# Second-stage matrix in four pieces, loads in shorter runs, and all projection tiles ahead of the last transform

## The chip, the cores and the metric

The kernel runs on one core of one Trainium2 chip. The metric is the device time of one execution, in microseconds. Names used below: TensorE (PE, matmul), VectorE (DVE), ScalarE (ACT), GpSimd (POOL) and SyncE (SP, which only issues transfers here).

## What is computed

The reference mixes two branches for a sequence of S = 2048 rows and D = 640 channels, with a gate for each row:

```python
x = A_q
g = sigmoid((x * gate_w).sum(-1, keepdims=True))
a = q * (causal_fft_conv(k_shift * v, ssm_k) + (k_shift * v) * ssm_D)     # FFT length 2*S
b = attention(x @ wqkv) @ wo          # 32 heads of 20, 8 keys at a distance of 2
return g * a + (1 - g) * b
```

k_shift is a four-tap convolution of k along the sequence. The long convolution is done with transforms written as matmuls: a first stage (F1b), a second stage (G), the product of the transformed filter h and the transformed data kv, then a first inverse stage (M) and a second inverse stage (T). The second branch is local attention with its output projection by wo.

## The kernel before

One program holds all parts, and a small list scheduler written into the kernel decides the order of instructions: each part is a generator that asks for an engine with an estimated cost and with events to wait for. The order is fixed when the program is built; each engine then works through its own stream in order. PSUM is divided into four slots; a part takes one or two of them and gives them back when the copy out of PSUM is done.

The loads, all issued by SyncE in this order (the part from the stores of kv on):

```python
yield from store_kv(3)
yield from store_kv(2)
yield from load_h(0)                     # first half of the filter, runs of 128 bytes
yield from store_kv(1)
yield from store_kv(0)
yield from load_h(1)                     # second half, 8 transfers
yield from load("G", G, cf["G"]..., 2097152, 16384, [ev("stg21"), ev("stg30"), ev("stg31")])
for c in range(2):
    yield from load(f"kv{c}", kvs[:, 5120 * c:5120 * (c + 1)], ..., 1310720, 10240, stored)
yield from load("wo", ...)
```

G lies in the tile Gs, which earlier holds staging for the q and k projections; GpSimd copies that staging by DMA into the head-wise tiles qb and kb ("fragger"). `stg21`, `stg30` and `stg31` are the events that the last of those copies are done.

A second-stage unit of the transform (there are 4 for each of 5 groups, for the filter "h" and for the data "u"):

```python
def s2_unit(dst, jb, Am, deps, free):
    r = yield Req("P", 680.0, deps + [ev("G")], take=1)
    ps = psum(r, "s2")
    for jj in range(8):
        j = 8 * jb + jj
        for rr in range(2):
            for c in range(2):
                ...
                nc.tensor.matmul(o, lhsT=G[rows, j, rr, :], rhs=Am[rows, 2 * j + rr, :, :], ...)
    e = yield Req("AD", n=1024, deps=[r.done, free], give=r.banks)     # copy out, ScalarE or VectorE
```

The load of q (for the product with the gate) and its scaling, the second inverse stage, and the output projection:

```python
def load_q():
    yield Req("G", 1.0, [ev("us1")])              # after the last reader of kv, whose place qg takes
    for g in range(4):
        r = yield Req("G", 700.0, move=us(655360, 20480))
        nc.gpsimd.dma_start(st["qg"][32 * g:32 * g + 32], raw(x2, 16 * g * D, [[64 * D, 32], [1, 16 * D]]))
    mark("qg", r)

def qscale():                                     # 16 tiles, VectorE: q times the gate
    for t in range(16):
        r = yield Req("D", 230.0, [ev("qg"), ev("gate")])
        ...

def inverse2():                                   # groups of 3 tiles: 96 matmuls, then two copies and two products
    for t0 in range(0, 16, 3):
        g = yield Req("P", m * 32 * 16.0, [ev("Cm"), ev("T"), ev("qg"), ev("gate")], take=2)
        ...

def outproj():                                    # 16 tiles of 40 matmuls
    for t in range(16):
        late = [ev(f"pr{t}")] if t >= EARLY else []        # EARLY = 12
        g = yield Req("P", 1510.0, late, take=1, pri=None if t < EARLY else 0)
        ...                                       # copy out times (1 - gate) into bl
        # t < 12: added two tiles at a time by early_adds; t >= 12: added one by one, then stored
```

So the last four projection tiles stand behind the second inverse stage; `pr{t}` is the event that tile t has its product with q.

Of the kernel before, what the change touches and what calls it, by code (L numbers as in the profile page):

```python
# [12 lines left out]
ACT = mybir.ActivationFunctionType  # L13
ALU = mybir.AluOpType
# [3 lines left out]
S = 2048  # L18
D = 640
# [16 lines left out]
GROUPS = [[0, 1, 2, 3], [4, 5, 6, 7], [8, 9, 10], [11, 12, 13], [14, 15, 16]]  # L36
PARTS = [((0, 1), [(0, 8)]), ((2, 3, 4), [(8, 5), (13, 4)])]

EARLY = 12
AHEAD = 2  # L40

NG = 5
# [179 lines left out]
def kernel(  # L222
# [105 lines left out]
    def loads():  # L328
# [45 lines left out]
        yield from load("G", G, cf["G"].ap().rearrange("p (a r b) -> p a r b", a=32, r=2), 2097152, 16384,  # L374
                        [ev("stg21"), ev("stg30"), ev("stg31")])
        stored = [ev(f"st{a}{c}") for a in range(4) for c in range(2)]
        for c in range(2):
            yield from load(f"kv{c}", kvs[:, 5120 * c:5120 * (c + 1)], raw(kv_scr[:], c * 4 * S * 80, [[5120, 128], [1, 5120]]), 1310720, 10240, stored)
# [291 lines left out]
        return e.done  # L670

    def s2_unit(dst, jb, Am, deps, free):
        r = yield Req("P", 680.0, deps + [ev("G")], take=1)
        ps = psum(r, "s2")
        for jj in range(8):
            j = 8 * jb + jj
            for rr in range(2):
                for c in range(2):
                    rows = slice(64 * c, 64 * c + 64)
                    o = ps[:, c, :].rearrange("p (q j l) -> p q j l", q=4, j=8)[:, :, jj, :]  # L680
                    nc.tensor.matmul(o, lhsT=G[rows, j, rr, :], rhs=Am[rows, 2 * j + rr, :, :],  # L681
                                     start=(rr == 0), stop=(rr == 1), tile_position=(64 * c, 0), skip_group_check=True)
# [222 lines left out]
    def outproj():  # L905
        yield Req("G", 1.0, [ev("oT"), ev("wo"), ev("gate")])
        oT, wo, bl = st["oT"], st["wo"], st["bl"]
        for t in range(16):
            late = [ev(f"pr{t}")] if t >= EARLY else []
            g = yield Req("P", 1510.0, late, take=1, pri=None if t < EARLY else 0)  # L910
            op = psum(g, "op", (128, 1024))
            for ft in range(NDT):
                a = oT[:, ft, 0:1]
                for n0, n1 in ((0, 512), (512, 640)):
                    for gg in range(4):
                        nc.tensor.matmul(op[32 * gg:32 * gg + 32, n0:n1],  # L916
                                         lhsT=raw(a, HS * (t % 2) + t // 2 + 8 * gg, [a.ap[0], [32, 32]]), rhs=wo[:, ft, n0:n1],
                                         start=(ft == 0), stop=(ft == NDT - 1), tile_position=(0, 32 * gg), skip_group_check=True)
            r = yield Req("AD", dict(A=725.0, D=880.0), [g.done] + late, give=g.banks)
            if t >= EARLY and r.eng == "D":  # L920
                qg = st["qg"]
                nc.vector.scalar_tensor_tensor(qg[:, t, :], op[:, 0:D], omg[:, t:t + 1], qg[:, t, :], op0=ALU.mult, op1=ALU.add)
            else:
                if r.eng == "A":
                    nc.scalar.activation(bl[:, t, :], op[:, 0:D], ACT.Copy, scale=omg[:, t:t + 1])  # L925
                else:
                    nc.vector.tensor_scalar(bl[:, t, :], op[:, 0:D], omg[:, t:t + 1], None, ALU.mult)
                if t >= EARLY:
                    qg = st["qg"]
                    yield Req("D", 410.0, [r.done])  # L930
                    nc.vector.tensor_tensor(qg[:, t, :], qg[:, t, :], bl[:, t, :], ALU.add)
            mark(f"bl{t}", r)
            if t >= EARLY and t % 2 == 1:
                store(t)
# [38 lines left out]
    plan.add(load_t(), 0)  # L973
    plan.add(load_q(), 1)
    plan.add(qscale(), 4)
    plan.add(early_adds(), 2)
    plan.add(inverse2(), 0)
    plan.run()

# [29 lines left out]
```

## Time and profile before

The time before is 275.25 us, the median of 3 runs (273.52 to 278.2). The profiled execution has a span of 273.6 us.

| stretch of the span, us | TensorE busy | VectorE | ScalarE | granted clock | DMA share |
|---|---|---|---|---|---|
| 84 to 104 | 18.91 of 20.00 | 10.69 | 18.69 | 1.00 | 0.67 |
| 104 to 114.6 | 8.26 of 10.60 | 7.90 | 10.11 | 0.71 | 0.97 |
| 114.6 to 122.7 | 0.08 of 8.10 | 0.62 | 1.58 | 0.50 | 0.99 |
| 122.7 to 147 | 22.04 of 24.30 | 16.91 | 19.64 | 0.50 | 0.24 |
| 147 to 160 | 9.03 of 13.00 | 8.58 | 9.46 | 0.76 | 0.99 |
| 212 to 226 | 10.97 of 14.00 | 7.75 | 9.35 | 0.95 | 0.60 |
| 226 to 240 | 12.22 of 14.00 | 10.65 | 9.39 | 0.93 | 0.30 |
| 240 to 252 | 6.11 of 12.00 | 7.50 | 7.50 | 0.71 | 0.28 |
| 252 to 262 | 8.62 of 10.00 | 5.44 | 5.04 | 0.67 | 0.61 |

The table is made from the busy time of each engine in stretches of the span. The granted clock is the share of full speed at which TensorE was let run. The DMA share is how busy the 16 transfer engines were. Transfers that matter here, from issue to landing: G 14.0 us (2048 KB), kv 17.5 us (median of two, 1280 KB each), q 11.1 us (median of four, 640 KB each), the filter 4.1 us (median of sixteen, 160 KB each).

How to read the profile's lines: a timeline row gives the start, the duration, the engine, the line of the program, the operation, what it writes and reads (out<-in), its shape and how many instructions are merged; in square brackets stands the idle time of the engine ahead of it and what ended that ("<-issue" where nothing that the profile shows was waited for). The chain of work that ended last is followed back from the last instruction.

### The profile page before, as it was taken

To read this page: it belongs to the slowest core of one execution; us is meant where nothing else is said; L and a number is where in the kernel's file an instruction comes from. 1 tells how busy PE (TensorE), PEld (TensorE's weight loads), DVE (VectorE), ACT (ScalarE), POOL (GpSimd) and SP (SyncE) were. 2 spreads that over 40 slices of the span, in tenths; PEclk is the share of its full clock that TensorE was granted. 3 is DMA by queue.
4 is the path that set the end of the run, shared out by engine and by line. 5 is a ranking of instruction groups with operands and counts; after the bars stand their busy time and mean duration, and the time that the engine had idled before them with its cause. 6 is when DMAs were issued, how large, how long until landed. Compare 5 with 4: busy or idle time off the path is not lost.

```text
span 273.6 us, 10626 instructions
## 1 busy us (share of the span) xinstructions
PE 219.5 (80%) x4825; PEld 164.2 (60%) x4825; DVE 178.0 (65%) x224; ACT 180.3 (66%) x219; POOL 59.5 (22%) x123
## 2 busy tenths in 40 slices
PE   1899999999999998508989496979999959845920
PEld 1675665555656666407869395868787848833510
DVE  0289189999998546606678566867749558747520
ACT  1155567887887999907888642867979755666420
POOL 7701534760702374200000000000000200012420
PEclk9999999999999999555555959999999998995595
DMA  6999899868930698997004966510400196005640
GB/s 202 300 376 415 279 224 74 203 176 158 211 84 14 185 158 148 272 333 298 7 2 98 230 145 151 128 32 5 156 6 2 41 206 143 2 18 127 145 110 0
DMA packets 40525, 40.11 MB, mean 147 GB/s; under 512 B 26544, under 2 KB 35888, under 8 KB 39200
## 3 DMA queue, kind: packets, MB, share of 16 engines
q1 hardware_dynamic: 36208, 29.41, 40.8%
q0 software_dynamic: 4272, 10.02, 16.0%
q8 instruction: 38, 0.62, 1.0%
q14 instruction: 7, 0.06, 0.1%
HBM read 23.50 MB, written 5.25 MB: 105 GB/s over the span
## 4 chain that ended last, share of the span: by engine, by line
PE 58%; issue 11%; DVE 11%; DMA 8%; ACT 7%; POOL 1%; POOLq 0%; SPq 0%; DVEq 0%; ACTq 0%
PE pj L530 12%; PE psv L478 8%; PE op L916 8%; PE i L808 7%; PE s L681 7%; DMA Gs<-cf_G 5%; DVE Am L251 4%; PE s L663 4%; ACT ET L604 3%; PE O L630 3%; PE sc L596 3%; PE tr L831 2%; PE trx L460 2%; DVE X L794 2%; DVE Hs L791 2%
## 5 line engine op out<-in xcount | busy, mean ns | idle before, releaser
L604 ACT ACTIVATE ET<-sc 128x726 bf16<-128x726 f32 (+1 forms) x80 | 64.3, 865 | 10.9 <-PE sc L596 10.6
L530 PE MATMUL pj<-xT,Wqk 128*128 128x363 bf16 (+3 forms) x250 | 48.2, 343 | 0.6 <-DVE oS L644 0.6
L681 PE MATMUL s<-Am,Gs 64*128 64x64 bf16 x1280 | 31.3, 205 | 19.6 <-issue 10.8
L681 PEld LDWEIGHTS <-Gs 64*128 64x128 bf16 x1280 | 27.4, 105 | 24.5 <-issue 14.8
L251 DVE CAST Am<-s 128x1024 bf16<-128x1024 f32 x27 | 32.4, 1222 | 13.0 <-PE s L663 12.9
L530 PEld LDWEIGHTS <-Wqk 128*128 128x128 bf16 x250 | 23.0, 97 | 19.0 <-DVE oS L644 0.8
L916 PE MATMUL op<-wo,Hb 128*32 128x512 bf16 (+1 forms) x640 | 27.4, 323 | 2.2 <-issue 1.5
L478 PE MATMUL psv<-Wv,xT 128*128 128x320 bf16 x170 | 26.7, 309 | 1.6 <-DVE xT L251 1.0
L249 ACT CAST X<-i 128x1024 bf16<-128x1024 f32 x20 | 20.2, 1012 | 9.3 <-PE i L808 9.3
L846 POOL DMA_DIRECT2D qg<-in_A_q_dram x4 | 2.0, 509 | 101.8 <-PE s L681 101.8
L916 PEld LDWEIGHTS <-Hb 128*32 128x32 bf16 x640 | 17.8, 139 | 9.1 <-issue 4.5
L808 PE MATMUL i<-M,X 128*128 128x128 bf16 x160 | 22.1, 233 | 0.4 <-DVE X L794 0.4
L478 PEld LDWEIGHTS <-xT 128*128 128x128 bf16 x170 | 16.4, 100 | 8.7 <-issue 1.7
L808 PEld LDWEIGHTS <-X 128*128 128x128 bf16 x160 | 21.0, 152 | 0.7 <-DVE X L794 0.7
L596 PE MATMUL sc<-qb,kb 31*128 31x121 bf16 x544 | 19.3, 242 | 2.3 <-ACT ET L604 1.2
L925 ACT ACTIVATE bl<-op,omg 128x640 bf16<-128x640 f32 x16 | 12.8, 802 | 9.7 <-PE op L916 9.7
L566 POOL DMA_DIRECT2D qb<-Gs x21 | 10.5, 505 | 38.7 <-ACT Gs L249 20.7
L808 PE MATMUL i<-M,Hs 128*128 128x128 bf16 x128 | 18.4, 236 | 0.0
L249 ACT CAST Gs<-pj 128x968 bf16<-128x968 f32 (+5 forms) x18 | 13.5, 749 | 7.3 <-PE pj L530 7.2
L630 PEld LDWEIGHTS <-ET 128*128 128x128 bf16 x544 | 15.9, 100 | 3.8 <-issue 2.1
L444 DVE TENSOR_TENSOR pa<-pa,pb 128x2560 bf16<-128x2560 bf16 x12 | 17.9, 1489 | 0.3
L630 PE MATMUL O<-VW,ET 128*128 128x21 bf16 x544 | 16.6, 176 | 1.6 <-ACT ET L604 1.2
(73 smaller groups left out, 372.5 us busy)
## 6 DMA issues: line engine op xcount, KB each, us to landing
X<-Hs SPq DMA_DIRECT2D x8, 512.0 KB, 7.4
xS<-in_A_q_dram SPq DMA_DIRECT2D x4, 640.0 KB, 8.9
Hb<-in_A_k_dram SPq DMA_DIRECT2D x4, 640.0 KB, 12.1
kv<-in_A_v_dram SPq DMA_DIRECT2D x4, 640.0 KB, 13.8
kv_scr<-Hb SPq DMA_DIRECT2D x8, 320.0 KB, 5.3
Hb<-in_A_ssm_k_dram SPq DMA_DIRECT2D x16, 160.0 KB, 4.1
kv<-kv_scr SPq DMA_DIRECT2D x2, 1280.0 KB, 17.5
qg<-in_A_q_dram POOLq DMA_DIRECT2D x4, 640.0 KB, 11.1
```

What stands on the lines that cost most here:

```text
L249: nc.scalar.copy(dst, src)
L251: nc.vector.tensor_copy(dst, src)
L444: nc.vector.tensor_tensor(pa[:], pa[:], pb[:], ALU.add)
L478: nc.tensor.matmul(ps[:, bb, 0:320], lhsT=xT[:, dt, BP * (b0 + bb):BP * (b0 + bb) + 128], rhs=Wv[:, dt, c0:c0 + 320], start=(dt == 0), sto ...
L530: nc.tensor.matmul(ps[:, i, 0:n], lhsT=Wqk[:, dt, w, 128 * ft:128 * ft + 128], rhs=rhs, start=(dt == 0), stop=(dt == NDT - 1))
L596: nc.tensor.matmul(scs[h4 // 2][:, h4 % 2, BP * bb:BP * bb + BP], lhsT=kb[r:r + DH + NF, 128 * b:128 * b + 128], rhs=qb[r:r + DH + NF, BP ...
L604: nc.scalar.activation(ETs[e][:, :, 0:nw], scs[hf][:, :, 0:nw], ACT.Exp, scale=SCALE)
L630: nc.tensor.matmul(O[:, o0:o0 + 21], lhsT=ET[:, hh, BP * bb:BP * bb + 128], rhs=VW[:, b, 4 * t + h4, :], start=True, stop=True, skip_group ...
L681: nc.tensor.matmul(o, lhsT=G[rows, j, rr, :], rhs=Am[rows, 2 * j + rr, :, :], start=(rr == 0), stop=(rr == 1), tile_position=(64 * c, 0), ...
L808: nc.tensor.matmul(o, lhsT=src[:, c, :, :, 8 * oc + il].rearrange("p q j -> p (q j)"), rhs=M[:, k, :], start=(k == 0), stop=(k == 1), skip ...
L916: nc.tensor.matmul(op[32 * gg:32 * gg + 32, n0:n1], lhsT=raw(a, HS * (t % 2) + t // 2 + 8 * gg, [a.ap[0], [32, 32]]), rhs=wo[:, ft, n0:n1] ...
L925: nc.scalar.activation(bl[:, t, :], op[:, 0:D], ACT.Copy, scale=omg[:, t:t + 1])
```

## The change

It does four things. G is loaded in four pieces, one for each second-stage unit of a group, ahead of the second half of the filter, and each unit waits for its own piece only. kv is read back in eight transfers with runs of 2,560 bytes instead of two with runs of 10,240. q is loaded in sixteen transfers with runs of 5,120 bytes (before: four, 20,480), tile group by tile group, alternating between SyncE and GpSimd, and scaling waits for its own group. All sixteen projection tiles lose the wait for the second inverse stage, so that the scheduler is free to put them ahead of it or between its groups; all additions are done two tiles at a time. The purpose is to have G there when its first reader comes, to keep long runs of data from holding up other traffic of the transfer engines, and to leave nothing but the second inverse stage for the end. The scheduler's model of the transfer pipe also starts 1 us later, and it is told 5 us more for each piece of G; both only move its estimates.

```diff
-EARLY = 12
@@ class Plan
-        self.pipe = 0.0
+        self.pipe = 1000.0
@@ loads
         yield from store_kv(0)
+        for jb in range(4):
+            yield from load(f"G{jb}", Gs[:, 2048 * jb:2048 * (jb + 1)], cf["G"].ap()[:, 2048 * jb:2048 * (jb + 1)], 524288, 4096,
+                            [ev("stg21"), ev("stg30"), ev("stg31")])
+            ev(f"G{jb}").t += 5000.0
         yield from load_h(1)
-        yield from load("G", G, ..., 2097152, 16384, [ev("stg21"), ev("stg30"), ev("stg31")])
         for c in range(2):
-            yield from load(f"kv{c}", kvs[:, 5120 * c:5120 * (c + 1)], ..., 1310720, 10240, stored)
+            for m in range(4):
+                yield from load(f"kv{c}", kvs[:, 5120 * c + 1280 * m:5120 * c + 1280 * (m + 1)], ..., 327680, 2560, stored)
@@ s2_unit
-        r = yield Req("P", 680.0, deps + [ev("G")], take=1)
+        r = yield Req("P", 680.0, deps + [ev(f"G{jb}")], take=1)
@@ load_q
-        for g in range(4):
-            r = yield Req("G", 700.0, move=us(655360, 20480))
-            nc.gpsimd.dma_start(st["qg"][32 * g:32 * g + 32], raw(x2, 16 * g * D, [[64 * D, 32], [1, 16 * D]]))
-        mark("qg", r)
+        for a in range(4):
+            for g in range(4):
+                r = yield Req("SG"[g % 2], 520.0, move=us(163840, 5120) * 1.5)
+                (nc.sync, nc.gpsimd)[g % 2].dma_start(st["qg"][32 * g:32 * g + 32, 4 * a:4 * a + 4, :]..., ...)
+            mark(f"qg{a}", r)
@@ qscale
-            r = yield Req("D", 230.0, [ev("qg"), ev("gate")])
+            r = yield Req("D", 230.0, [ev(f"qg{t // 4}"), ev("gate")])
@@ inverse2
-            g = yield Req("P", m * 32 * 16.0, [ev("Cm"), ev("T"), ev("qg"), ev("gate")], take=2)
+            g = yield Req("P", m * 32 * 16.0, [ev("Cm"), ev("T"), ev(f"qs{t0 + m - 1}")], take=2)
@@ outproj
-            late = [ev(f"pr{t}")] if t >= EARLY else []
-            g = yield Req("P", 1510.0, late, take=1, pri=None if t < EARLY else 0)
+            g = yield Req("P", 1510.0, take=1)
 ...        # the branch for t >= EARLY (add and store tile by tile) is removed
-    def early_adds():
-        for t in range(1, EARLY, 2):
+    def adds():
+        for t in range(1, 16, 2):
             yield Req("D", 740.0, [ev(f"bl{t}"), ev(f"pr{t}")])
```

(Cut to its core; lines shortened with "...".)

More of the change, by code (lines that the diff above doesn't have):

```diff
@@ L372, in loads @@
         yield from store_kv(0)
+        for jb in range(4):
+            yield from load(f"G{jb}", Gs[:, 2048 * jb:2048 * (jb + 1)], cf["G"].ap()[:, 2048 * jb:2048 * (jb + 1)], 524288, 4096,
+                            [ev("stg21"), ev("stg30"), ev("stg31")])
+            ev(f"G{jb}").t += 5000.0
         yield from load_h(1)
-        yield from load("G", G, cf["G"].ap().rearrange("p (a r b) -> p a r b", a=32, r=2), 2097152, 16384,
-                        [ev("stg21"), ev("stg30"), ev("stg31")])
         stored = [ev(f"st{a}{c}") for a in range(4) for c in range(2)]
         for c in range(2):
-            yield from load(f"kv{c}", kvs[:, 5120 * c:5120 * (c + 1)], raw(kv_scr[:], c * 4 * S * 80, [[5120, 128], [1, 5120]]), 1310720, 10240, stored)
+            for m in range(4):
+                yield from load(f"kv{c}", kvs[:, 5120 * c + 1280 * m:5120 * c + 1280 * (m + 1)],
+                                raw(kv_scr[:], c * 4 * S * 80 + 1280 * m, [[5120, 128], [1, 1280]]), 327680, 2560, stored)
         wo = p0.tile([128, NDT, D], BF, name="wo", tag="wo")
@@ L843, in load_q @@
         st["qg"] = qg
-        for g in range(4):
-            r = yield Req("G", 700.0, move=us(655360, 20480))
-            nc.gpsimd.dma_start(st["qg"][32 * g:32 * g + 32], raw(x2, 16 * g * D, [[64 * D, 32], [1, 16 * D]]))
-        mark("qg", r)
+        for a in range(4):
+            for g in range(4):
+                r = yield Req("SG"[g % 2], 520.0, move=us(163840, 5120) * 1.5)
+                (nc.sync, nc.gpsimd)[g % 2].dma_start(st["qg"][32 * g:32 * g + 32, 4 * a:4 * a + 4, :].rearrange("p t c -> p (t c)"),
+                                                      raw(x2, (16 * g + 4 * a) * D, [[64 * D, 32], [1, 4 * D]]))
+            mark(f"qg{a}", r)
     def load_t():
@@ L918, in outproj @@
                                          start=(ft == 0), stop=(ft == NDT - 1), tile_position=(0, 32 * gg), skip_group_check=True)
[L919 to L922, printed above, removed]
-            else:
[L924 to L931, printed above, removed]
+            r = yield Req("AD", dict(A=725.0, D=880.0), [g.done], give=g.banks)
+            if r.eng == "A":
+                nc.scalar.activation(bl[:, t, :], op[:, 0:D], ACT.Copy, scale=omg[:, t:t + 1])
+            else:
+                nc.vector.tensor_scalar(bl[:, t, :], op[:, 0:D], omg[:, t:t + 1], None, ALU.mult)
             mark(f"bl{t}", r)
-            if t >= EARLY and t % 2 == 1:
-                store(t)
-    def early_adds():
-        for t in range(1, EARLY, 2):
+    def adds():
+        for t in range(1, 16, 2):
             yield Req("D", 740.0, [ev(f"bl{t}"), ev(f"pr{t}")])
@@ L975 @@
     plan.add(qscale(), 4)
-    plan.add(early_adds(), 2)
+    plan.add(adds(), 2)
     plan.add(inverse2(), 0)
```

## The prediction

> **What bounds the kernel now.** I read the page's slices first, then the chain of work that ended last, then the timeline of TensorE wherever the chain says "DMA" or "issue", and last the timelines of the queues that feed those places. In the page, the rows show the busy share of TensorE, its granted clock and the DMA engines; below them stand the instruction queue and the chain.
>
> ```profile
> PE   1899999999999998508989496979999959845920
> PEclk9999999999999999555555959999999998995595
> DMA  6999899868930698997004966510400196005640
> q8 instruction: 38, 0.62, 1.0%
> PE 58%; issue 11%; DVE 11%; DMA 8%; ACT 7%; POOL 1%; POOLq 0%; SPq 0%; DVEq 0%; ACTq 0%
> ```
>
> TensorE carries most of the chain, but there is one empty slice (the eighteenth, DMA at 9), several dips, and a thin end. "issue" at 11% is large. The empty slice, in TensorE's timeline:
>
> ```profile
> 114.15 0.52 PE L596 MATMUL sc<-qb,kb 31*128 31x121 bf16 x12 [0.34 <-DVE oS L644]
> 122.69 1.03 PE L681 MATMUL s<-Am,Gs 64*128 64x64 bf16 x32 [8.02 <-DMA Gs<-cf_G]
> ```
>
> The first second-stage unit waits 8.02 us for the matrix G, and since the stream is in order, all scores behind it wait too. Why so late? SyncE's queue, then GpSimd's:
>
> ```profile
> 95.43 12.82 SPq L331 DMA_DIRECT2D Hb<-in_A_ssm_k_dram  x8
> 108.61 0.77 SPq L331 DMA_DIRECT2D Gs<-cf_G  x1
> ...
> 97.12 1.00 POOL L566 DMA_DIRECT2D qb<-Gs  x2 [5.85 <-PE sc L596]
> 98.11 1.00 POOL L566 DMA_DIRECT2D kb<-Gs  x2
> ```
>
> G is issued at 108.61, behind the eight loads of the filter's second half, which hold the queue for 12.82 us; it then needs 14.0 us to land (page, DMA issues). But G overwrites the staging space of the projections, and the last readers of that space are the two GpSimd rows, issued by 99.1. G could start several microseconds earlier.
>
> Now the "issue" rows of TensorE, the waits that no semaphore explains, and the thin end:
>
> ```profile
> 224.84 0.90 PE L681 MATMUL s<-Am,Gs 64*128 64x64 bf16 x27 [3.03 <-issue]
> ...
> 240.34 1.50 PE L881 MATMUL i<-X,T 32*32 32x160 bf16 x148 [1.10 <-ACT X L249]
> 243.71 1.34 PE L881 MATMUL i<-X,T 32*32 32x160 bf16 x128 [1.86 <-issue]
> 247.16 1.74 PE L881 MATMUL i<-X,T 32*32 32x160 bf16 x110 [2.12 <-issue]
> 249.45 0.45 PE L881 MATMUL i<-X,T 32*32 32x160 bf16 x18 [0.55 <-ACT X L890]
> 250.89 1.43 PE L881 MATMUL i<-X,T 32*32 32x160 bf16 x108 [0.99 <-issue]
> 252.99 1.72 PE L916 MATMUL op<-wo,Hb 128*32 128x512 bf16 x20 [0.66 <-ACT X L890]
> 255.17 6.58 PE L916 MATMUL op<-wo,Hb 128*32 128x128 bf16 x140 [0.47 <-issue]
> ```
>
> Between two of these stops lie 128, then 110+18 = 128, then 108+20 = 128 matmuls, each with its weight load: 256 instructions. They resume at 243.71, 247.16, 250.89 and 255.17, so 3.45, 3.73 and 4.28 us apart. I read them as waits for the next block of instructions.
>
> **What the skill says.** "Runtime: NRT & Kernel Launch", Instruction fetch mechanics: an engine's program is fetched in blocks of 256 instructions, the next during the current one, and crossing is mostly hidden. The trace agrees on the size (38 packets, 0.62 MB, so 16.3 KB each; stops 128 pairs apart) and not on "mostly hidden" here. "DMA: Bandwidth & Descriptors", Queues, rings and completion order: an engine goes round its queues packet by packet. If so, a fetch waits behind long runs of data. The trace supports this only indirectly: the 3.03 us stop falls into the load of q, whose runs are 20,480 bytes. "TensorE: Matmul & The Clock Gate", What's actually happening: idle time halves the clock. The granted clock is indeed 0.50 from about 109 to 147, but it falls before the wait for G, so I book nothing for the clock.
>
> **The change part by part.**
>
> G in four pieces, ahead of the second half. In the built SyncE stream the four loads now stand right behind the last kv store (89.9). Piece 0 overwrites only staging whose readers were issued by 72.7 and can go at once. Pieces 1 to 3 need the GpSimd rows at 97 to 99; those small transfers took 3 to 6 us, so they go at 101 to 105. 1.5 MB at G's old rate, 2 MB in 14.0 us = 0.146 MB/us, is 10 us; with the filter's 128-byte runs no longer beside them, rather 6 to 8, so they land at 109 to 113. The first piece is wanted at 114.7, the others one by one over several microseconds. The wait of 8.02 should go. The filter's half is issued afterwards, 103 to 115, landing before about 120; its first reader is the eleventh first-stage unit (143.46 before, 8 us less is 135). So it is hidden. Also, the scheduler now puts more of attention ahead of the transform: before the last attention product there stand nine first-stage and four second-stage units, where before there were eleven and seven. In 122.7 to 147 TensorE was busy 22.0 of 24.3 us at half clock and ScalarE 19.6, so attention ends some 2 us sooner than by the shift alone, and five units come later at full clock, about 1.1 us for a pair. Net: perhaps +1. **Gain 8.0 + 1.**
>
> kv in short runs. First read at 170.98; issued by 110.3, landing within 17.5 us, so at about 128. **0** by itself; its fetch relief falls at 110 to 128, when TensorE now runs where it stood still: blocks can run out there under full DMA. I take **-1.5**.
>
> q in short runs, tile by tile, on two queues. Same 2.6 MB. The stop of 3.03 us at 221.8 lies on the chain. The block before it began about 217.6 and the next came at 224.84, 7.2 us for what takes 3.45 at the quiet end; consumption of a block took 4.2. With 5,120-byte runs the fetch should fit 4 to 5 us. **Gain 2** of 3.03. New: four of the sixteen scalings by the gate (4.83/16 = 0.30 us each) now stand ahead of the last product group on VectorE. VectorE is idle there (222.7 to 225.8 before) and q's first tiles, 640 KB, should have landed by then.
>
> Last transform. Before: from 225.75, 64 matmuls (5.1 us), two projection tiles (4.2 with a stop of 1.03), 64 matmuls throttled by four ScalarE copies of 1.01, first i2 matmul at 240.34: 14.6 us. After: 48 matmuls (3.8), one tile (1.5), 16 (1.3), 64 of the last group (4.5; its products end at 231.8, in time), last copy 1.1: 12.2 us, the second tile lying beside the copy. **Gain 2.4**, I take 2.
>
> End. Before: from 240.34 to VectorE's last addition at 263.11 is 22.8 us, with TensorE in two phases: i2 limited by copies and fetch, then four tiles. After: tile and i2 group alternate. Same 512 + 160 = 672 matmuls, same place in the blocks. With the fetch as above (first resume after 3.4, then 3.45 + 3.73 + 4.28 = 11.5, a block of 1.7, and the last 12 behind one more fetch) the last matmul stands at 3.4 + 11.5 + 3.5 = 18.4. Then two short copies, products and one addition (0.82): about 1.7. Sum 20.1. From ScalarE's timeline (copies of 0.97, the last two 0.27 each, tiles 0.80) it needs 10 x 0.97 + 2 x 0.27 + 4 x 0.80 = 13.4; VectorE, with ten products of 0.66, two short ones and eight additions of 0.82, about 13.6: neither binds before the fetch. **Gain 2.7.**
>
> Sum: 8 + 1 - 1.5 + 2 + 2 + 2.7 = 14.2 us. 275.25 - 14.2 = 261.0.
>
> **The rivals.** (1) *The fetch takes G's place.* Pairs of 8 + 32 matmuls in about 1 us use a block in 3.2 us, no more than a quiet fetch; running earlier only means waiting for blocks. For it: stops of 3.09, 2.31 and 1.45 at 154, 168 and 179 beside the swaps. Then half of G's gain is lost: about 266. (2) *G's pieces wait as well*, because pieces 2 and 3 hold SyncE's queue for the staging readers and then h, kv and wo pile up behind them. Against it: everything behind has 15 us or more of slack. It would give 264 to 267. (3) *VectorE blocks on q.* If q's first tiles land later than 225, the last products, and the end, move by as much: 2 to 4 us. (4) *The end is bound by copies*: alternating tiles share the four PSUM slots with i2, which takes two at a time; then its gain is 0 to 1. (5) Everything works and attention stays ahead with a warmer clock: 256.
>
> **Range and chances.** One wait of 8 us is certain in the trace and its cure is well founded; even with half the rest lost the result is near 268, and 2% is 269.7. Range 256 to 269. Faster by over 2%: 0.90; within: 0.07; slower: 0.03.
>
> **What would show it.** The 8.02 row for G gone or under 1 us; SyncE issuing G's last piece by about 105 and the filter's half after; the last attention product near 135 rather than 146. The issue stop beside q under 1.5 us. From the first i2 matmul to the last addition about 20 us. The prediction is wrong if new issue rows fill 110 to 130, if the scaling row waits for q ahead of the last products, or if the instruction stops at the end grow with the stores beside them.

## The result and the profile after

The changed kernel takes **262.06 us** (median of 4 runs, 260.87 to 265.50) against 274.75 us for the kernel before on the same chip (4 runs, 273.52 to 278.2). The ratio is 0.9538, with a 95% interval from 0.9474 to 0.9602. A second comparison, told below, gave a smaller gain: 0.9746 (0.9682 to 0.9809). The kernel before scatters by up to 8.6 us from run to run on one chip, so a single profile is good to a few microseconds. Ratios, and the gains over the kernel before that follow from them, leave out slow runs (over 1.5% above the fastest run of the same kernel), while the medians given with each kernel hold all its runs.

The rows of the page after that answer to those shown of before (busy share of TensorE, its granted clock, the transfer engines, the instruction queue, the chain of work that ended last):

```profile
PE   1899999999999999778879567989989979986400
PEclk9999999999999999955557999999999997999955
DMA  6999899968990184998957984600400097015530
q8 instruction: 37, 0.61, 1.1%
PE 55%; DVE 22%; issue 9%; ACT 8%; DMA 2%; POOL 1%; POOLq 0%; SPq 0%; ACTq 0%; DVEq 0%
```

The empty slice of TensorE is gone, DMA has fallen from 8% of the chain to 2%, and "issue" is still 9%. The dip of the clock lasts four slices in a row, not six. In the timeline of TensorE, kernel after:

```profile
114.93 0.52 PE L599 MATMUL sc<-qb,kb 31*128 31x121 bf16 x12 [0.34 <-DVE oS L647]
115.64 1.03 PE L684 MATMUL s<-Am,Gs 64*128 64x64 bf16 x32 [0.18 <-ACT ET L607]
...
213.19 0.59 PE L684 MATMUL s<-Am,Gs 64*128 64x64 bf16 x29 [1.67 <-issue]
...
226.63 1.02 PE L886 MATMUL i<-X,T 32*32 32x160 bf16 x96
...
229.73 0.94 PE L886 MATMUL i<-X,T 32*32 32x160 bf16 x86 [0.36 <-issue]
...
233.73 1.00 PE L886 MATMUL i<-X,T 32*32 32x160 bf16 x94 [1.38 <-ACT bl L925]
...
237.46 0.49 PE L920 MATMUL op<-wo,Hb 128*32 128x512 bf16 x6 [1.27 <-issue]
...
241.19 0.76 PE L920 MATMUL op<-wo,Hb 128*32 128x512 bf16 x14 [1.10 <-issue]
...
244.92 0.28 PE L886 MATMUL i<-X,T 32*32 32x160 bf16 x14 [1.79 <-issue]
```

The first second-stage unit waits 0.18 us for a copy of attention instead of 8.02 us for G. The stop beside the load of q is 1.67 us instead of 3.03. In the end, projection tiles and the last transform now alternate, but the stops are still there. TensorE goes on at 229.73, 233.73, 237.46, 241.19 and 244.92: 4.00, 3.73, 3.73 and 3.73 us apart. The timeline of SyncE's queue (start, time that the queue was held, what is written):

```profile
90.30 12.92 SPq L330 DMA_DIRECT2D Gs<-cf_G  x4
103.38 17.96 SPq L330 DMA_DIRECT2D Hb<-in_A_ssm_k_dram  x8
```

The last piece of G is issued by 103.2, and the second half of the filter goes behind it. Where the span became shorter, from the same marks in both timelines of TensorE (the last one in VectorE's):

| stretch | before, us | after, us | gained |
|---|---|---|---|
| start to first first-stage unit of the filter | 104.61 | 104.75 | -0.1 |
| to first second-stage unit | 18.08 | 10.89 | 7.2 |
| to end of last attention product | 23.59 | 20.12 | 3.5 |
| to first unit on kv | 24.70 | 25.26 | -0.6 |
| to first matmul of the first inverse stage | 16.08 | 16.09 | 0.0 |
| to first matmul of the last transform | 53.28 | 49.54 | 3.7 |
| to end of last addition | 22.77 | 21.23 | 1.5 |

These 15.3 us belong to two single executions; the medians differ by 12.7. In a second profile of the changed kernel the stretch to the first unit on kv is 27.26 instead of 25.26, so that 2 us of the gain vanish between two executions of one program.

### The profile page after: what moved, and what is told of

The parts are those of the page before. It is cut to its first block, busy times and chain, and to the rows that moved or that the text cites. A ratio compares the mean times of both kernels' runs of the same rounds, so it can differ in the third digit from the quotient of the medians.

```text
span 258.9 us, 10662 instructions
## 1 busy us (share of the span) xinstructions
PE 213.2 (82%) x4825; PEld 159.2 (62%) x4825; DVE 176.8 (68%) x221; ACT 181.0 (70%) x220; POOL 61.2 (24%) x127
## 4 chain that ended last, share of the span: by engine, by line
PE 55%; DVE 22%; issue 9%; ACT 8%; DMA 2%; POOL 1%; POOLq 0%; SPq 0%; ACTq 0%; DVEq 0%
PE psv L481 9%; PE i L811 9%; PE op L920 8%; PE s L684 7%; PE pj L533 6%; DVE pa L447 5%; DVE pb L432 5%; ACT ET L607 5%; PE O L633 4%; PE s L666 3%; PE sc L599 3%; PE trx L463 2%; PE i L886 2%; PE tr L834 2%; DVE Am L250 2%
## 5 line engine op out<-in xcount | busy, mean ns | idle before, releaser
L250 DVE CAST Am<-s 128x1024 bf16<-128x1024 f32 x25 | 30.0, 1220 | 10.6 <-PE s L666 10.5
L684 PE MATMUL s<-Am,Gs 64*128 64x64 bf16 x1280 | 29.3, 199 | 9.2 <-issue 7.3
L684 PEld LDWEIGHTS <-Gs 64*128 64x128 bf16 x1280 | 25.3, 101 | 13.8 <-issue 12.0
L920 PE MATMUL op<-wo,Hb 128*32 128x512 bf16 (+1 forms) x640 | 26.2, 305 | 2.4 <-issue 2.4
L850 POOL DMA_DIRECT2D qg<-in_A_q_dram x8 | 3.9, 500 | 82.4 <-PE s L684 82.4
L811 PE MATMUL i<-M,X 128*128 128x128 bf16 x160 | 22.7, 236 | 0.2 <-DVE X L797 0.2
L920 PEld LDWEIGHTS <-Hb 128*32 128x32 bf16 x640 | 16.5, 136 | 8.5 <-issue 3.0
L811 PEld LDWEIGHTS <-X 128*128 128x128 bf16 x160 | 21.2, 152 | 0.4 <-DVE X L797 0.4
L599 PE MATMUL sc<-qb,kb 31*128 31x121 bf16 x544 | 18.5, 242 | 2.1 <-ACT ET L607 1.0
L248 ACT CAST X<-s 128x1024 bf16<-128x1024 f32 x17 | 17.0, 1012 | 3.3 <-PE s L684 2.4
L811 PE MATMUL i<-M,Hs 128*128 128x128 bf16 x128 | 19.1, 241 | 0.0
```

Source lines behind the costliest of these rows:

```text
L248: nc.scalar.copy(dst, src)
L250: nc.vector.tensor_copy(dst, src)
L599: nc.tensor.matmul(scs[h4 // 2][:, h4 % 2, BP * bb:BP * bb + BP], lhsT=kb[r:r + DH + NF, 128 * b:128 * b + 128], rhs=qb[r:r + DH + NF, BP ...
L811: nc.tensor.matmul(o, lhsT=src[:, c, :, :, 8 * oc + il].rearrange("p q j -> p (q j)"), rhs=M[:, k, :], start=(k == 0), stop=(k == 1), skip ...
L920: nc.tensor.matmul(op[32 * gg:32 * gg + 32, n0:n1], lhsT=raw(a, HS * (t % 2) + t // 2 + 8 * gg, [a.ap[0], [32, 32]]), rhs=wo[:, ft, n0:n1] ...
```

## The experiments

The kernels ran in three groups of four; those of a group shared the chip and the runs of the kernel before (medians 273.45, 273.70 and 274.29 us). The kernel after ran again in the second group alone, so kernels of the other two are set against it by their ratios to before. In most of the profiles the first first-stage unit comes at 106.4 to 107.4 instead of 104.6 to 104.8 us, with a granted clock of 0.89 instead of 1.00 between 30 and 45 us. This happens to one and the same program in one execution and not in another, so marks are compared from that unit on.

### What is G's place in the queue worth?

First theory: the wait for G was 8 us of the path, and its removal gives about 7.5 us to the end. Rival: the instruction stream, or another wait, takes back half of it. **G alone** (the kernel before with G's four pieces ahead of the filter's half):

```diff
-        self.pipe = 0.0
+        self.pipe = 1000.0
         yield from store_kv(0)
+        for jb in range(4):
+            yield from load(f"G{jb}", Gs[:, 2048 * jb:2048 * (jb + 1)], ...)
+            ev(f"G{jb}").t += 5000.0
         yield from load_h(1)
-        yield from load("G", G, ...)
-        r = yield Req("P", 680.0, deps + [ev("G")], take=1)
+        r = yield Req("P", 680.0, deps + [ev(f"G{jb}")], take=1)
```

> The kernel before, with G alone changed: four pieces ahead of the filter's second half, each unit waiting for its own piece (the scheduler then also puts attention further ahead). Theory (G's wait and the attention order are two thirds of the gain): about 264.5 us, ratio 0.96; first second-stage unit at about 115.6 without a wait for G, last attention product near 135.7, the end of the program as before (first matmul of the last transform to the last addition 22 to 23 us). Rival (what is won at G is given back in stops for instructions behind it): 268 or more, with over 5 us of unexplained stops between 110 and 161.

Measured: 269.09 us (267.66 to 270.32), ratio 0.9888 (0.9799 to 0.9976): **3.1 us** (by the interval 0.7 to 5.5), not 7.5. "Issue" stops of TensorE between 110 and 161 us add up to 5.4 us, as the rival has it, where before has one of 3.1. The profiles alone would mislead here: from the first first-stage unit to the last addition, G alone takes 151.0 us and before takes 158.5, but these two profiles come from different groups, and the kernel before has no profile of this group. Nor is it known whether its runs here have the late start of the profile of G alone, from which up to 2 us of the difference may come.

**The new order alone** (the kernel after, its stream of TensorE unchanged, but G sent as one load behind the filter's half):

```diff
         for jb in range(4):
-            yield from load(f"G{jb}", ...)
+            g = yield Req("S", 300.0 + 64.0, [ev("stg21"), ev("stg30"), ev("stg31")], move=us(524288, 4096))
+            mark(f"G{jb}", g)            # for the scheduler's estimates only
             ev(f"G{jb}").t += 5000.0
         yield from load_h(1)
+        nc.sync.dma_start(G, cf["G"].ap().rearrange("p (a r b) -> p a r b", a=32, r=2))
```

> The kernel after, with G loaded in one piece behind the filter's second half as before, while the order of TensorE's instructions stays exactly that of after. Theory (the transfer's place in the queue is the cause): the wait for G is back with 7 to 8 us at the first second-stage unit, the time about 269, ratio 0.98. Rival (the scheduler's other order is the cause, the place of the load only lets it come about): the wait is under 3 us or the time stays below 264.5.

Measured: 267.19 us (265.53 to 268.47), ratio 0.9816 (0.9733 to 0.9900): 5.0 us less than before although the wait for G is still there whole; what else the change holds (order, q, the end) does that.

**G whole, but ahead** (the kernel after with one load of 2 MB in place of the four pieces):

```diff
-        for jb in range(4):
-            yield from load(f"G{jb}", Gs[:, 2048 * jb:2048 * (jb + 1)], ...)
-            ev(f"G{jb}").t += 5000.0
+        yield from load("G", G, ..., 2097152, 16384, [ev("stg21"), ev("stg30"), ev("stg31")])
+        ev("G").t += 5000.0
         yield from load_h(1)
```

> The kernel after, with G as one load of 2 MB ahead of the filter's second half; same order on TensorE. It must wait for the last reader of the whole staging space (about 102 to 103). Theory A (being ahead of the filter is enough): it lands by 114 to 116, the wait for G is 0 to 1.5 us, time 262 to 263.5. Theory B (the pieces matter, since the first may land 10 us earlier and the first unit needs no other): a wait of 2 to 6 us, time 264 to 268.

Measured: 264.89 us (263.72 to 265.32), ratio 0.9728 (0.9659 to 0.9798). The timelines of TensorE show both halves of the answer. With the new order and G behind the filter:

```profile
125.64 1.03 PE L685 MATMUL s<-Am,Gs 64*128 64x64 bf16 x32 [8.19 <-DMA Gs<-cf_G]
...
158.41 0.23 PE L685 MATMUL s<-Am,Gs 64*128 64x64 bf16 x4 [2.21 <-issue]
158.69 0.66 PE L685 MATMUL s<-Am,Gs 64*128 64x64 bf16 x32
```

With G whole, ahead of the filter:

```profile
117.23 1.04 PE L683 MATMUL s<-Am,Gs 64*128 64x64 bf16 x32 [0.18 <-ACT ET L606]
...
132.98 0.54 PE L632 MATMUL O<-VW,ET 128*128 128x21 bf16 x14 [0.99 <-issue]
...
152.66 0.29 PE L683 MATMUL s<-Am,Gs 64*128 64x64 bf16 x4 [2.75 <-issue]
153.17 1.06 PE L683 MATMUL s<-Am,Gs 64*128 64x64 bf16 x32
```

The place in the queue is the cause of the wait: 8.19 us with G behind, 0.18 with G ahead. No worth of the four pieces can be seen: the first second-stage unit stands 10.2 us behind the first first-stage unit with one load, 10.9 and 10.2 in the two profiles with four, and the ratio to before is 0.9728 with one and 0.9746 with four (in another group). But of the 8 us only 2.3 reach the end in the medians (267.19 - 264.89; the runs of the two do not overlap). In the two timelines, counted from the first first-stage unit, the lead of the early G is 8.0 us at the first second-stage unit, 6.1 at the end of attention, 4.4 at the first unit on kv, 4.2 at the first inverse stage, 4.0 at the last transform and 2.8 at the last addition.

Part of what is given back can be named. Up to the end of attention, the kernel with G early has 1.6 us of "issue" stops (0.60 and 0.99), the one with G late none. The trace's records of the transfers show why. TensorE's program comes in packets of 16,384 bytes on the instruction queue, one for each block of 256 instructions. In the 8.19 us of standing still (117.45 to 125.64) one packet came; packets, MB and share of the engines' time:

```profile
q8 instruction: 1, 0.02, 0.9%
```

It landed at 121.01. The next one started at 130.74, 2.4 us after TensorE had begun on the block that this one brought. So instructions did not pile up during the wait: one block was ready, and that spared the late kernel the stop of 0.60. The stop of 0.99 has another reason. The same stretch, from the first second-stage unit to the end of attention, first with G late, then with G early (length, then TensorE, weight loads, VectorE, ScalarE, GpSimd, with the number of instructions, granted clock, DMA share, GB/s):

```profile
125.64:144.57 18.93, 16.70 (x472) 13.74 (x474) 13.82 (x19) 16.52 (x21) 0.00 (x0) 0.50 0.36 132
```

```profile
117.23:138.06 20.83, 17.02 (x472) 13.73 (x473) 14.23 (x20) 17.96 (x23) 0.57 (x1) 0.50 0.84 222
```

With G late, most of G and of kv moves while TensorE stands still (DMA share 0.96 in those 8.19 us). With G early, the filter's half and kv move beside attention, at a DMA share of 0.84 instead of 0.36. The packet for the stop of 0.99 starts 3.1 us after the block ahead of it was begun; the packet of the same block starts after 1.1 us with G late.

Behind attention comes the stop of 2.75 instead of 2.21 us, and in the 5.9 us behind it the granted clock is 0.53; the late one has 0.70 in the 5.6 us behind its own stop. The group of 32 matmuls takes 1.06 us in one, at a granted clock of 0.50, and 0.66 us in the other, at 0.88. What is lost after the first unit on kv (1.6 us) is no more than two executions of one kernel differ by, and I leave it unexplained.

A last attempt was to keep **the old order with G early** (the kernel before; the four pieces are sent ahead of the filter's half, while the scheduler is still told that G comes behind):

```diff
         yield from store_kv(0)
+        for jb in range(4):
+            nc.sync.dma_start(Gs[:, 2048 * jb:2048 * (jb + 1)], cf["G"].ap()[:, 2048 * jb:2048 * (jb + 1)])
         yield from load_h(1)
-        yield from load("G", G, ..., 2097152, 16384, [ev("stg21"), ev("stg30"), ev("stg31")])
+        g = yield Req("S", 300.0 + 64.0, [ev("stg21"), ev("stg30"), ev("stg31")], move=us(2097152, 16384))
+        mark("G", g)
```

> The kernel before, with G in four pieces ahead of the filter's second half and nothing else: TensorE, VectorE and ScalarE keep the order of before. Theory (the transfer's place alone removes the wait): no wait for G, first second-stage unit 10.5 us behind the first filter unit instead of 18.1; from there to the last attention product 23.6 as before; the time 4 to 6 us under before. Rival (the gain needs the order): 0 to 3 us. If the order of attention is worth something of its own, the kernel with G and the order (20 us from that unit to the last attention product) is the faster of the two by 1 us or more.

Measured: 271.56 us (268.87 to 274.66), ratio 0.9894 (0.9799 to 0.9988). It does not answer the question. The loads now stand in the program ahead of six of the copies that read the staging, so these copies wait for G and carry G's numbers: some heads work on other data than the reference's. The timeline of GpSimd shows what that costs:

```profile
106.15 0.99 POOL L568 DMA_DIRECT2D kb<-Gs  x2 [13.37 <-DMA Gs<-cf_G]
```

Attention then lacks its keys and ends 27.4 us behind the first second-stage unit (23.59 before). So how much the order of attention brings with G early was not measured by itself.

### q and the order of the last inverse

Theory: short runs of q let the instructions through (2 us), and the new order ahead of the last transform brings 2 more. **q in long runs** (the kernel after with q's four loads of before):

```diff
+        for g in range(4):
+            r = yield Req("G", 700.0, move=us(655360, 20480))
+            nc.gpsimd.dma_start(st["qg"][32 * g:32 * g + 32], raw(x2, 16 * g * D, [[64 * D, 32], [1, 16 * D]]))
         for a in range(4):
-            for g in range(4):
-                r = yield Req("SG"[g % 2], 520.0, move=us(163840, 5120) * 1.5)
-                (nc.sync, nc.gpsimd)[g % 2].dma_start(...)
             mark(f"qg{a}", r)
```

> The kernel after, with q in four transfers with runs of 20,480 bytes on GpSimd alone, as before; the scheduler, told so, puts the projection tiles ahead of the last inverse group as before and leaves two transform groups at the end without a tile between. Theory (long runs hold up the fetch of instructions, and the later q costs the order): the unexplained stop beside the load of q grows from 1.7 to 2.5 to 3 us, the stretch from the first matmul of the first inverse stage to the first of the last transform from 49.5 to 52 or more, the time 2 to 4 us over that of after on this chip. Rival (length of the runs is of no matter, q being read late): stop and time as in after within 1 us.

Measured: 267.77 us (266.47 to 271.14), ratio 0.9886 (0.9826 to 0.9946).

Beside it ran **the kernel after once more**, unchanged:

> The changed kernel once more, as the yardstick for the other three of this group on the same chip. Both theories: ratio to before 0.954 within 0.01, first second-stage unit without a wait for G.

Measured: 263.64 us (262.33 to 264.67), ratio 0.9746 (0.9682 to 0.9809): 6.9 us less than before. The ratio was expected at 0.954 within 0.01; it is outside, and a gain of 2% lies just inside its interval. Against the kernel with long runs the split load of q is worth 4.1 us. The stop in the timeline of TensorE with long runs:

```profile
216.37 0.59 PE L684 MATMUL s<-Am,Gs 64*128 64x64 bf16 x29 [2.79 <-issue]
```

The same place has 1.10 in the second profile of the kernel after. Much of the rest is order: without an event for each quarter of q, the scheduler puts 64 matmuls of the first inverse, two tiles, and 64 more, as before, where the kernel after has one tile between 48 and 16. The stretch from the first inverse to the last transform is 54.0 us instead of 49.8. The two terms were not measured apart: the kernel with long runs also has another order.

**q in runs of one row**, 1,280 bytes, with an identical order of instructions:

```diff
-dma_start(st["qg"][32 * g:32 * g + 32, 4 * a:4 * a + 4, :].rearrange("p t c -> p (t c)"), raw(..., [[64 * D, 32], [1, 4 * D]]))
+dma_start(st["qg"][32 * g:32 * g + 32, 4 * a:4 * a + 4, :], raw(..., [[64 * D, 32], [D, 4], [1, D]]))
```

> The kernel after, with q's sixteen transfers in runs of 1,280 bytes instead of 5,120; nothing else differs, all engines have the same instructions in the same order. If long runs hold up the fetch packet by packet: the stop beside q falls from 1.7 to 1 us or less, the time falls by 0 to 1 us. If the fetch is held up by the amount of data in flight and not by the length of runs: the stop stays at 1.5 to 2 us, or grows because short runs move slower.

Measured: 263.69 us (261.17 to 265.50), ratio 0.9724 (0.9648 to 0.9800), the same as after. Over all profiles, the stop beside q is 2.5 to 3.3 us with runs of 20,480 bytes (four kernels), 0.85 to 2.16 with 5,120 (eight profiles of seven kernels), 1.11 with 1,280 (one). The means are 2.9 and 1.6 us, so some 1.3 us of it goes with the load of before. The records of the transfers show where: the packet of instructions that ends the stop starts 2.8 to 3.5 us after the block ahead of it was begun with 20,480 bytes, 1.3 to 2.7 with 5,120 and 1.8 with 1,280; it is then on its way for 1.0 to 1.4 us in all of them, and TensorE goes on 1.35 to 1.6 us after it has landed. So the packet is held up before it starts. The load of before also differs in the number of transfers and in being sent by GpSimd alone, so that the length of the runs alone is not shown to be the cause; below 5,120 bytes it made no difference.

**Swaps in shorter runs**, 1,024 bytes: the exchange of the halves of the filter's spectrum, beside which other stops lie (5.4 us in sum between the last attention product and the first unit on kv, 6.1 in the second profile):

```diff
-            nc.sync.dma_start(Hw[0:64], Hs[64:128])
+            nc.sync.dma_start(Hw[0:64].rearrange("p c q j l -> p (c q) (j l)"), Hs[64:128].rearrange("p c q j l -> p (c q) (j l)"))
             # and the same for the other half
```

> The kernel after, with the ten transfers that swap the halves of the filter's spectrum (512 KB each) in runs of 1,024 bytes instead of 8,192; instructions and order are the same. If long runs hold up the fetch: the stops between the last attention product and the first data unit (5.4 us in sum in after) fall to 3 us or less and the time falls by 1 to 3 us. If it is the amount in flight, or the blocks are used faster than a quiet fetch brings them (3.4 us for 128 pairs): sum and time stay within 1 us.

Measured: 265.69 us (263.39 to 268.06), ratio 0.9805 (0.9719 to 0.9890). The time is no shorter. The stops add up to 4.2 us, neither the 3 or less of the one theory nor the sum of after; and a kernel with the swaps of after (the one with half a transform, below) has 3.0 there, so the stops of single profiles decide nothing.

**kv in long runs** (the kernel after with the two loads of before, runs of 10,240 bytes):

```diff
-            for m in range(4):
-                yield from load(f"kv{c}", kvs[:, 5120 * c + 1280 * m:5120 * c + 1280 * (m + 1)], ..., 327680, 2560, stored)
+            yield from load(f"kv{c}", kvs[:, 5120 * c:5120 * (c + 1)], ..., 1310720, 10240, stored)
```

> The kernel after, with kv read back in two transfers with runs of 10,240 bytes as before; the same order on TensorE. Theory (kv is read 30 us after it lands, its runs matter only to the fetch): time within 1 us of after; the stops ahead of the last attention product grow from 0.8 to 1.5 us to 2 to 3. Rival (the short runs are worth more than that): 2 us or more over after, with a wait for kv or for the filter's second half.

Measured: 264.86 us (262.01 to 265.89), ratio 0.9665 (0.9584 to 0.9746). The stops ahead of the last attention product add up to 2.9 us (0.8 and 1.5 in the two profiles of the kernel after). But the kernel with q in long runs, whose kv runs are short, has 2.9 there as well, so this is not shown to come from kv. In the time no loss can be seen: the ratio is not above that of the kernel after, 0.9746, which ran in another group.

### What bounds the end?

Theory: TensorE waits there for blocks of 256 instructions, which come at their own pace. Rival: the copies out of PSUM bind, and the stops only look like a fetch. **The stream moved by 64 pairs**: 64 matmuls, whose results nothing reads, are added behind those of the gate, early in the program. A fetch moves its stops by 64 pairs against the work; copies do not.

```diff
-        gps = psum(g, "gps", (128, 16))
+        gps = psum(g, "gps", (128, 32))
+        for k in range(64):
+            nc.tensor.matmul(gps[:, 16 + k % 16:17 + k % 16], lhsT=xT[:, 0, ...], rhs=wg[:, 0:1], start=True, stop=True)
         ...                          # the copy behind reads gps[:, 0:16] as before
```

> The kernel after, with 64 additional small matmuls behind the gate's (they write PSUM columns that nobody reads), so that everything behind them stands 64 pairs further on in TensorE's stream; order otherwise the same. If the unexplained stops are waits for blocks of 256 instructions: they move by 64 pairs ahead in the content, so in the last transform they stand not at pairs 146, 402, 530 and 658 from its first matmul but at 82, 210, 338, 466 and 594 or some of these, and still 128 apart. If they come from transfers, PSUM or the work itself: they stay at the same pairs or times. The time rises by 1 to 3 us in both cases.

Measured: 268.41 us, a single run, so no interval. The last transform in the timeline of TensorE:

```profile
237.34 0.84 PE L888 MATMUL i<-X,T 32*32 32x160 bf16 x74
238.85 0.32 PE L888 MATMUL i<-X,T 32*32 32x160 bf16 x22 [0.67 <-issue]
239.10 1.59 PE L922 MATMUL op<-wo,Hb 128*32 128x512 bf16 x40
240.62 0.78 PE L888 MATMUL i<-X,T 32*32 32x160 bf16 x66
242.85 0.35 PE L888 MATMUL i<-X,T 32*32 32x160 bf16 x30 [1.46 <-issue]
...
246.85 0.54 PE L888 MATMUL i<-X,T 32*32 32x160 bf16 x38 [1.49 <-issue]
...
250.31 0.91 PE L888 MATMUL i<-X,T 32*32 32x160 bf16 x78 [0.83 <-issue]
```

Counted from the first matmul of the last transform, the stops of the kernel after stand ahead of pairs 146, 274, 402, 530 and 658, each 128 behind the last. Here they stand at 210 (96 + 40 + 74), 338 (22 + 40 + 66 later), 466 and 594: the same places moved by 64. Also the stop at 233.73 of the kernel after, which the profile puts down to a copy, is the one at pair 274 of this row. TensorE goes on here 4.00, 4.00 and 3.46 us apart.

The records of the transfers of the kernel after show the fetches themselves:

| packet starts, us | on its way, us | TensorE goes on at, us | after landing, us | next packet starts, us later |
|---|---|---|---|---|
| 227.39 | 0.93 | 229.73 | 1.41 | 1.12 |
| 230.85 | 1.38 | 233.73 | 1.50 | 1.13 |
| 234.86 | 1.11 | 237.46 | 1.49 | 1.12 |
| 238.58 | 1.24 | 241.19 | 1.38 | 1.13 |
| 242.32 | 1.28 | 244.92 | 1.32 | |

Each step is a round: TensorE begins on a block, 1.1 us later the packet of the next one starts, it is on its way for about 1.2 us, and 1.3 to 1.5 us after it has landed the first matmul of that block runs. The stop at 233.73 goes with a packet like the others, so the copy named beside it did not end it.

**Half of the last transform's matmuls.** The kernel leaves out the imaginary half of the last transform, 256 matmuls; copies, products and additions remain as many.

```diff
-                for r in range(2):
+                for r in range(1):
-                        start=(r == 0), stop=(r == 1), ...
+                        start=True, stop=True, ...
```

> The kernel after, with half the matmuls of the last transform left out (the imaginary half of its sum, 256 matmuls; the copies and products stay, the output lacks that half). If the end is bound by the fetch of instructions (two blocks fewer, 3.5 us each): from its first matmul to the last addition 21.2 falls to 15 to 16.5. If it is bound by copies and products (ScalarE 13.4 us of work, VectorE 13.6, in step with each other): it falls to 19 at the lowest.

Measured: 257.81 us (256.23 to 258.76), ratio 0.9418 (0.9355 to 0.9481). Busy time of each engine from the first matmul of the last transform to the last addition, first in the second profile of the kernel after, then in this kernel (length, then TensorE, weight loads, VectorE, ScalarE, GpSimd, with the number of instructions, granted clock, DMA share, GB/s):

```profile
229.80:251.03 21.23, 12.66 (x680) 8.87 (x672) 13.47 (x20) 13.62 (x17) 6.34 (x13) 0.99 0.38 97
```

```profile
230.56:245.77 15.21, 9.80 (x424) 7.55 (x416) 12.84 (x20) 12.79 (x17) 6.34 (x13) 0.93 0.49 132
```

With the same 17 instructions of ScalarE and 20 of VectorE the stretch is 6.0 us shorter, and no "issue" stop is left in it. The time is 7.1 us less than that of the kernel with kv in long runs, of the same group. TensorE had only 2.9 us of work less. So the copies do not bind in the kernel after; here they nearly do (12.8 of 15.2 us). The theory of the fetch holds, the rival falls.

**The last four tiles late**, as in the kernel before, all else as after:

```diff
+EARLY = 12
+            late = [ev(f"pr{t}")] if t >= EARLY else []
-            g = yield Req("P", 1510.0, take=1)
+            g = yield Req("P", 1510.0, late, take=1, pri=None if t < EARLY else 0)
             # and, for t >= EARLY, added and stored tile by tile as in the kernel before
```

> The kernel after, with the last four projection tiles behind the second inverse stage as before; the rest of TensorE's order as in after. Theory: only the end gives back, 1.5 to 2.5 us, so 263.5 to 264.5; first matmul of the last transform to last addition 22 to 23 us instead of 21.2. Rival (alternating tiles and transform groups is worth nothing, since copies and PSUM slots bind): the same 262 within 0.5.

Measured: 265.56 us (263.57 to 266.72), ratio 0.9735 (0.9643 to 0.9828). Behind the first matmul of the last transform it takes 23.63 us, 2.4 more than after. That is above the 263.5 to 264.5 and the 22 to 23 us expected. But in time it can't be told from the kernel with G whole and all tiles early, 264.89 on the same chip: tiles that stand late are not done early, and the last transform starts 0.8 us sooner in its profile, counted from the first first-stage unit.

## Why the prediction was right, step by step

The prediction was 261.0 us in a range of 256 to 269, with 0.90 for faster by over 2%. 262.06 and, in the second comparison, 263.64 lie inside. The gain is over 2% in the first; in the second it is 2.5% with an interval from 1.9 to 3.2. The reasons held in direction; the sizes of two parts did not.

- **The block of G, 8.0 + 1 - 1.5 = 7.5 us: mis-sized.** Its mechanism is right: the row of 8.02 us is gone, the last piece of G was issued by 103.2 ("by about 105"), the last attention product ended at 135.8 ("near 135"). But the whole block alone gives 3.1 us in the time (0.9888 is the ratio, and 7.5 us would be 0.972, outside its interval), and G's place alone, in the new order, 2.3. The failing step is the term of -1.5 for what the 8 us give back. For the stretch it was taken for it was good: up to the end of attention the early G has 1.6 us of "issue" stops with one load, and 1.5 and 0.8 in the two profiles of the kernel after. It left out what lies behind: of the 8.0 us of lead, 1.9 are gone at the end of attention, another 1.7 at the first unit on kv, and another 1.6 at the last addition, 5.2 in all. This is the size of the **first rival**, "half of G's gain is lost", which put the result near 266. Its mechanism, a fetch that takes G's place, is shown for the 1.6 us alone; the cause of the rest stays open in part. The +1 for the order of attention was not measured alone.
- **Second rival (G's pieces hold the queue): half seen, harmless.** The second half of the filter was issued from 103.4 to 121.3, 18 us rather than the 12 worked out, and no reader waited for it on the path.
- **kv, 0: not contradicted.** Long runs of kv cost nothing that the time shows.
- **q and the order of the last inverse, 2 + 2: right as a sum**, 4.1 us measured. The stop fell by 1.4 us in the first profile and 1.9 in the second (predicted: under 1.5 left; 1.67 and 1.10 were). One reading behind it was off: the block ahead of the stop began at 218.7, not about 217.6 (128 matmuls back from 224.84), so it took 6.1 us, 3.1 of them work, and not 7.2 and 4.2.
- **Third rival (VectorE blocks on q): true in small.** The timeline of VectorE, kernel after:

```profile
214.30 1.27 DVE L863 TENSOR_SCALAR qg<-qg,g_nat 128x640 bf16<-128x640 bf16 x4 [1.86 <-issue]
215.49 0.69 DVE L794 TENSOR_TENSOR sH<-X,sH 128x1024 bf16<-128x1024 bf16 x1
...
246.31 1.55 DVE L934 TENSOR_TENSOR qg<-qg,bl 128x1280 bf16<-128x1280 bf16 x2
```

  The four scalings are idle for 1.86 us ahead of their start at 214.30, and the last product starts at 215.49, though the copy that it needs ended at 214.88: 0.6 us lost, not 2 to 4.
- **The end, 2.7: partly.** The place of the last matmul was worked out as 18.4 us behind the first, and it ended at 18.57; the steps of 3.73 and 4.00 us between blocks carry it. The tail after it is 2.66 us, not 1.7, because two additions of two tiles each (1.55 us, the last row above) are left, not one. So the stretch is 21.2 instead of 20.1 us, 1.5 less than before, where 2.7 was predicted. In the time, the late tiles cost 0.7 us, less than these comparisons can resolve.
- **Fourth rival (copies bind the end): fallen**, by the moved stops, by the packets and by the halved transform. **Fifth (a warmer clock, 256): fallen**; the granted clock is 0.50 from 117.1 to 136.9 in the second profile too.

The measured parts are 3.1 for the block of G, 4.1 for q with its order, and 0.7 for the end: 7.9 us, beside 6.9 in the second comparison and 12.7 in the first. What the first has over this was not taken apart. So that 262.06 came so close to 261.0 is in part luck: the parts as measured alone, taken from 275.25, would have put it near 267. Since the kernel before scatters from 269.5 to 278.1 us in these runs, its median is the loosest number in the study. No version that holds the full computation is clearly faster than the kernel after; one load of G instead of four, q in runs of 1,280 bytes, or kv in long runs do as well.

## What to carry to other kernels

Ask of a wait that you remove not only how long it is but what else goes on during it: here, 8 us of waiting for data were also 8 us in which other transfers passed and one block of instructions came in, and only 2 to 3 us reached the end. Where many small matmuls stand in a row, count matmuls between "issue" stops. Equal counts point to a fetch, and the packets of the instruction queue in the trace confirm it. Then the number of instructions is the cost, not their work: here, 256 matmuls fewer took 6.0 us off, of which 2.9 were work. When loads are split, look at what the finer events let the scheduler do; that can be worth as much as the shorter transfer.

## What the runs showed of the hardware that I had not expected

The Trainium skill, "Runtime: NRT & Kernel Launch", Instruction fetch mechanics, has the crossing from one block of 256 instructions to the next mostly hidden. For the last transform the runs say otherwise: 128 matmuls with their weight loads, 40 of them of a projection tile, take some 2.6 us of TensorE (from 238.85 to 241.4 in the moved stream), and the next block comes 3.5 to 4.0 us after the last one, even with the DMA share at 0.38 (second profile of the kernel after). The reason is in the packets of the kernel after: the next one starts only 1.1 us after TensorE has begun on the block ahead of it, and a round of 3.7 to 4.0 us follows from its parts. In a wait of 8.19 us (G late, new order) one packet came, not two.

A stop of 2.75 us was followed by 5.9 us at a granted clock of 0.53. And the granted clock was 0.50 for 20 us in which TensorE was busy 16.87 of 19.88 us (second profile of the kernel after, 117.05 to 136.93), in attention and the first transform, without a wait of 8 us ahead of it; what holds it there stays open.
